# The second gather of an attention unit asked for one step later, and q loaded by ScalarE

## The chip, the cores and the metric

The kernel runs on one core of a Trainium2 chip. That core has five engines with an instruction stream each: TensorE (PE for its matmuls, PEld for its weight loads), VectorE (DVE), ScalarE (ACT), GpSimd (POOL) and SyncE (SP). Transfers between main memory and the core's memory run on 16 DMA engines; SyncE and ScalarE ask for plain ones, GpSimd for indirect ones (gathers). The metric is the device time of one execution in microseconds, smaller being better. A profile is of one further execution.

## The reference

Sparse attention, and then a layer of eight experts of which each row uses two:

```python
scores = scale * np.matmul(q, k.transpose(0, 1, 3, 2))     # batch 4, 8 heads, 768 rows, 64 wide
# a block of 32 rows sees its neighbours, the first and the last block, and 3 sampled blocks;
# the first and the last block of rows see everything
scores = np.where(mask, scores, -1000000000.0)
attn = softmax(scores)
x = np.matmul(attn, v)                                     # then rows of 512: 3072 x 512
logits = x @ w_gate
noisy_logits = logits + np.log1p(np.exp(x @ w_noise)) * noise
# the two best experts of a row, weights by a softmax over the two
h = np.maximum(x[mask] @ w1[e], 0.0)
out[mask] += top2_w[mask, k, None] * (h @ w2[e])
```

## The kernel before

Attention is cut into twelve units. A unit is a pair of batches and a group of 128 rows of each: six groups, two pairs. Five groups of a pair hold four blocks of 32 rows that see only eight blocks of keys each ("G"); one holds the first and last block (dense, "D") and two blocks more ("X"). A G unit has four macros: two batches times two halves of the heads. `Attention.steps` runs the macros as a pipeline, one step for each: in step n PE makes the scores of macro n (line 246, x32 matmuls), transposes the weights of macro n-1 (line 318), and multiplies those of macro n-2 with V (line 334, 64 matmuls, the groups named `va` and `vb` in turn). VectorE takes the row maxima of the scores (line 267) and norms the result (lines 376 to 382); ScalarE makes the exps (line 306) and copies the transposes (line 320). Routing of finished rows (lines 295 to 770) is slipped in between, in earnest from about step 28 on. After step 63 come the expert layers, which the change does not touch.

What a unit needs is fetched during the unit before it, by `ahead(n)`, which is called at the end of step n. For a G unit it consists of four gathers and four plain loads, and of keys and q:

- `gather_v(u, j)`, line 200: an indirect load of the sampled and near V rows of block j into `va`, 128 rows of 1040 floats, asked for by GpSimd. Ahead of each stands a 1x1 copy to `tick` (line 437) that reads VectorE's newest row maxima, so that GpSimd gets to the gather only when that step's maxima are made. `va` has two buffers, by the unit's parity; the first gather of a unit must wait until the unit before last has read its own.
- `load_v(u, j)`, line 194: a plain load of V windows into `vb`, asked for by ScalarE.
- `gather_k(u, bb)`, lines 211 to 216: twelve copies by GpSimd of sampled key blocks into `kg`, in the second step for the first batch and in the fourth for the second. `place_k` (line 236) is VectorE's part of it. The scores of the next unit read `kg`.
- `load_q(u)`, line 175: the q of the next unit, 512 KB, in the first step; `scale_q` (line 180) scales it on VectorE in the third.

Which gather stands in which step is set by `plan` (lines 414 to 421), where s is the first step of the unit that the V is for, so that s - 4 to s - 1 are the four steps of the unit before it. Every engine works its list in the order in which the program is written, and so does each queue of DMA requests. SyncE's list holds the finished rows (line 559, each waits for the norm), keys and V of the second pair of batches (lines 165 and 169), and q.

Of the kernel before, what the change touches and what calls it, by code (L numbers as in the profile page):

```python
# [40 lines left out]
class Attention:  # L41
# [130 lines left out]
    def load_q(self, k):  # L172
        hp, g = self.units[k]
        q = self.st["q", k] = self.qp.tile([P, self.BP, self.PR, P], F32, name="q")
        self.nc.sync.dma_start(q, self.qt[hp, g])

    def scale_q(self, k):

# [231 lines left out]
    def plan(self):  # L410

        self.values = {}
        for u in range(1, len(self.units)):
            s = self.first_step[u]
            for j in range(4):
                at = (s - 7 + 2 * j,) * 2
                if self.units[u - 1][1] != self.SPEC:
                    at = s - 3 + max(j - 1, 0), s - 3 + j
                for kind, n in zip("ab", at):
                    if kind == "b" or j < self.blocks(self.units[u][1]):  # L420
                        self.values.setdefault(n, []).append((kind, u, j))
# [1202 lines left out]
```

## Time and profile before

| what | us |
|---|---|
| median of three runs | 823.7 |
| lowest and highest | 817.61, 833.19 |
| profiled execution, its own time | 820.33 |
| its span, first to last instruction | 818.5 |
| attention's last steps end about | 283 |

The profile page gives each engine's busy time over the span. Further views group instructions by stretch, list them in order of time, or tell for one line how long its transfers took to land. In brackets behind a row of the timeline stands how long the engine was idle just before it and what ended that; "issue" there means that nothing the profile shows was waited for. The granted clock of TensorE is told as a share of 2.4 GHz; it has two levels, and 0.50 is the lower, 1.2 GHz.

### The profile page before, as it was taken

What the parts mean: (1) busy time and instruction counts of PE and PEld (TensorE: products, weight loads), DVE (VectorE), ACT (ScalarE), POOL (GpSimd) and SP (SyncE); (2) the same over time, 40 slices, a digit from 0 to 9 for tenths busy, and PEclk for the clock granted to TensorE, in tenths of its full rate; (3) what the DMA queues carried; (4) which work ended last, traced back from release to release, by engine and by line L of the source; (5) the groups of instructions that cost most, each with busy time, mean ns of one, the idle gap of its engine ahead of it and who ended that gap; (6) DMA issues with size and microseconds to landing.
All of it is one profiled execution on the core that took longest, in us unless ns stands there. A gap on an engine that the chain in (4) does not pass through costs nothing. (4 is left out here: it accounts for less than half of the span.)

```text
span 818.5 us, 21046 instructions
## 1 busy us (share of the span) xinstructions
PE 764.2 (93%) x8506; PEld 455.4 (56%) x8506; DVE 564.2 (69%) x1132; ACT 416.3 (51%) x729; POOL 333.7 (41%) x528
## 2 busy tenths in 40 slices
PE   5898989898998999999999999999999999999996
PEld 2566766775676775665445445444544544545542
DVE  5675659787897686426687786786787787785620
ACT  3574556455564542425375465554546546635620
POOL 4466565532366002423637327336335433333332
PEclk9999999899998899999999999999999999999999
DMA  9988788962486897979978378369359439343023
GB/s 358 341 278 285 246 310 289 324 222 67 134 260 213 169 326 255 184 177 164 286 143 222 89 126 235 95 111 222 85 84 236 132 65 190 99 100 48 1 41 56
DMA packets 122922, 148.66 MB, mean 182 GB/s; under 512 B 66111, under 2 KB 82751, under 8 KB 122816
## 3 DMA queue, kind: packets, MB, share of 16 engines
q1 hardware_dynamic: 97328, 75.76, 34.7%
q0 software_dynamic: 17600, 49.66, 25.3%
q10 hardware_dynamic: 7888, 21.81, 7.5%
q8 instruction: 69, 1.13, 0.5%
q14 instruction: 37, 0.30, 0.1%
HBM read 106.30 MB, written 27.00 MB: 163 GB/s over the span
## 5 line engine op out<-in xcount | busy, mean ns | idle before, releaser
L1160 POOL DMA_INDIRECT out_dram<-y,mt x56 | 85.7, 1530 | 260.7 <-ACT y L1155 121.2
L1099 PE MATMUL py<-w2h,hl 128*128 128x512 f16 x376 | 142.7, 380 | 0.8 <-DVE hl L1037 0.8
L1099 PE MATMUL py<-w2h,hh 128*128 128x512 f16 x376 | 142.8, 380 | 0.0
L1099 PE MATMUL py<-w2l,hh 128*128 128x512 f16 x376 | 142.7, 380 | 0.0
L1099 PEld LDWEIGHTS <-hh 128*128 128x128 f16 x752 | 72.9, 98 | 88.4 <-issue 2.5
L320 ACT ACTIVATE t<-t 128x512 f32<-128x512 f32 (+1 forms) x120 | 63.4, 568 | 80.3 <-PE t L318 79.7
L1055 PE MATMUL ph<-tx,w1a 128*128 128x408 f16 x384 | 99.0, 340 | 0.0
L1055 PEld LDWEIGHTS <-w1a 128*128 128x128 f16 x672 | 66.0, 98 | 58.0 <-issue 8.1
L1155 ACT ACTIVATE y<-py,r_tab 128x512 f32<-128x512 f32 (+1 forms) x49 | 33.6, 686 | 119.1 <-PE py L1099 102.1
L216 POOL COPY kg<-kv 128x128 f32 x264 | 68.4, 304 | 47.5 <-issue 15.1
L306 ACT ACTIVATE p<-s,nm 128x256 f32<-128x256 f32 x176 | 69.4, 480 | 25.5 <-DVE nm L267 24.8
L879 POOL TENSOR_TENSOR w2l<-wraw,w2h 128x1024 f16<-128x1024 f32 x24 | 51.7, 2152 | 62.5 <-ACT w2h L878 62.4
L318 PE MATMUL t<-ident,p 128*128 128x128 f32 x448 | 71.7, 302 | 4.9 <-ACT p L306 2.2
L960 POOL DMA_INDIRECT kv<-x_rows,gi x56 | 62.4, 1114 | 28.3 <-issue 12.1
L1037 DVE SCALAR_TENSOR_TENSOR hl<-ph,hh 128x408 f16<-128x408 f32 (+3 forms) x64 | 32.2, 525 | 58.3 <-ACT hh L1036 58.3
L318 PEld LDWEIGHTS t<-ident,p 128*128 128x128 f32 x448 | 52.1, 150 | 36.1 <-issue 16.6
L1036 ACT ACTIVATE hh<-area 128x408 f16<-128x408 f32 (+1 forms) x48 | 33.2, 713 | 72.6 <-DVE area L1059 72.6
L1055 PE MATMUL ph<-tx,w1b 128*128 128x408 f16 x192 | 65.2, 340 | 0.0
L1059 DVE TENSOR_TENSOR area<-ph,area 128x408 f32<-128x408 f32 x96 | 53.5, 578 | 15.7 <-PE ph L1055 11.1
L334 PE MATMUL po<-va,t 128*32 128x65 f32 x1408 | 49.5, 232 | 15.4 <-issue 8.7
L1099 PEld LDWEIGHTS <-hl 128*128 128x128 f16 x376 | 36.7, 98 | 45.6 <-DVE hl L1037 1.3
L267 DVE TENSOR_REDUCE nm<-s 128x4 f32<-128x1024 f32 (+1 forms) x48 | 54.2, 1129 | 8.5 <-PE s L246 8.4
(217 smaller groups left out, 1455.9 us busy)
## 6 DMA issues: line engine op xcount, KB each, us to landing
wraw<-in_moe_w_dram SPq DMA_DIRECT2D x64, 512.0 KB, 6.1
vb<-in_v_windows_dram ACTq DMA_DIRECT2D x16, 520.0 KB, 5.2
vb<-in_v_windows_dram ACTq DMA_DIRECT2D x24, 260.0 KB, 5.1
q<-in_q_dram SPq DMA_DIRECT2D x12, 512.0 KB, 9.0
out_dram<-zero ACTq DMA_DIRECT2D x8, 768.0 KB, 4.8
x_rows<-xr SPq DMA_DIRECT2D x19, 256.0 KB, 4.7
kv<-in_v_dram SPq DMA_DIRECT2D x2, 1560.0 KB
kv<-in_v_dram SPq DMA_DIRECT2D x6, 520.0 KB
```

The source lines that it names most:

```text
L216: nc.gpsimd.tensor_copy(KG[:, j, :, 32 * s:32 * s + 32], KT[:, :, bass.ds(offs[3 * j + s], 32)])
L267: red = lambda out, x: nc.vector.tensor_reduce(out, x, axis=AX.X, op=ALU.max, negate=True)
L306: self.nc.scalar.activation(p[:, 256 * u:256 * u + 256], S[:, a, 256 * r:256 * r + 256], AF.Exp, bias=nb[:, u:u + 1], scale=1.0 if k else ...
L318: self.nc.tensor.transpose(T[i][:, c:c + P], p[:, i * w + c:i * w + c + P], self.ident)
L320: self.nc.scalar.activation(t[:, i * w:(i + 1) * w], T[i][:, 0:w], AF.Copy)
L334: mm = lambda o, n, hl, l, r, start, stop: self.nc.tensor.matmul(O[o:o + n, hl], l, r, start=start, stop=stop, tile_position=(0, o))
L879: self.nc.gpsimd.tensor_tensor(lo, t, hi, op=ALU.subtract)
L960: g = nc.gpsimd.indirect_dma_start(out=self.xg[0:m, c], out_offset=None, in_=self.x_dram[0:nr], in_offset=bass.IndirectOffsetOnAxis(ap=r[" ...
L1055: nc.tensor.matmul(bank[:, 0:HC], self.wop[part][:, w, kb, fs], b(kb, a), start=start and n == 0, stop=n == 5, skip_group_check=True)
L1059: add = lambda e, out, p, q: e.tensor_tensor(out, p, q, op=ALU.add)
L1099: nc.tensor.matmul(py, h[:, f, o], w[x][:, f, :], start=i == 0, stop=i == last)
L1160: s = nc.gpsimd.indirect_dma_start(out=self.out, out_offset=bass.IndirectOffsetOnAxis(ap=r["mt"][0:m, c:c + 1], axis=0), in_=y[0:m], in_of ...
```

## The change

In `plan`, the steps of a G unit's gathers (those marked "a") become s-3, s-2, s-2, s-1 where they were s-3, s-3, s-2, s-1: the second gather is asked for in the third step of the unit before, not in its second. The plain V loads ("b") keep their steps, and so do the two units that follow a unit with dense rows. In `load_q` the loads of units 2 to 11 are asked for by ScalarE; those of units 0 and 1 stay with SyncE.

```diff
     def load_q(self, k):
         hp, g = self.units[k]
         q = self.st["q", k] = self.qp.tile([P, self.BP, self.PR, P], F32, name="q")
-        self.nc.sync.dma_start(q, self.qt[hp, g])
+        (self.nc.scalar if k > 1 else self.nc.sync).dma_start(q, self.qt[hp, g])
...
                 if self.units[u - 1][1] != self.SPEC:
-                    at = s - 3 + max(j - 1, 0), s - 3 + j
+                    at = s - 3 + (j + 1) // 2, s - 3 + j
```

GpSimd's list of before, in the second to fourth step of the first G unit (`tick` and `va` are the tick and the gather, line 211 loads the block numbers, 216 copies the keys; `nm` are a step's maxima, and the number tells the step):

```order
L437 COPY tick_100<-nm_876 1x1
L200 DMA va0_93<-in_v_dram,vidx_101 128x1040
L437 COPY tick_100<-nm_876 1x1
L200 DMA va0_93<-in_v_dram,vidx_101 128x1040
L211 TENSOR_LOAD koff_99
...
L437 COPY tick_100<-nm_988 1x1
L200 DMA va0_93<-in_v_dram,vidx_101 128x1040
L437 COPY tick_100<-nm_1069 1x1
L200 DMA va0_93<-in_v_dram,vidx_101 128x1040
L211 TENSOR_LOAD koff_99
```

GpSimd's list of the changed kernel at the same place:

```order
L437 COPY tick_100<-nm_876 1x1
L200 DMA va0_93<-in_v_dram,vidx_101 128x1040
L211 TENSOR_LOAD koff_99
...
L437 COPY tick_100<-nm_984 1x1
L200 DMA va0_93<-in_v_dram,vidx_101 128x1040
L437 COPY tick_100<-nm_984 1x1
L200 DMA va0_93<-in_v_dram,vidx_101 128x1040
L437 COPY tick_100<-nm_1069 1x1
L200 DMA va0_93<-in_v_dram,vidx_101 128x1040
L211 TENSOR_LOAD koff_99
```

One pair of tick and gather has moved from ahead of the first twelve key copies to behind them, and its tick reads the maxima of the third step.

ScalarE's list in the first step of a unit, as a piece of the difference (`q` is the moved load, `vb` the plain V load):

```order
 L306 ACTIVATE p<-s,nm 128x256 x4
 L194 DMA vb_95<-in_v_windows_dram 128x1040
+L175 DMA q<-in_q_dram 128x1024
 L320 ACTIVATE t<-t_1283 128x512
 L320 ACTIVATE t<-t_1284 128x512
```

The load of q stands behind the step's exps and V load and ahead of the next step's copies of transposes. From SyncE's list ten such loads are gone, each from behind finished rows and, in the first pair of batches, keys.

## Rows read from the trace of the kernel before

**Rows 1.** The page: busy time by engine, and the instruction queue (packets, MB, share).

```profile
PE 764.2 (93%) x8506; PEld 455.4 (56%) x8506; DVE 564.2 (69%) x1132; ACT 416.3 (51%) x729; POOL 333.7 (41%) x528
...
q8 instruction: 69, 1.13, 0.5%
```

**Rows 2.** Busy time by stretch: engines, then TensorE's clock, DMA share, GB/s.

```profile
0.00:180.00 180.00, 152.84 (x3586) 113.95 (x3587) 124.99 (x336) 95.08 (x216) 97.01 (x289) 0.94 0.85 298
...
135.00:152.00 17.00, 14.74 (x412) 11.42 (x413) 16.41 (x53) 9.43 (x23) 11.92 (x31) 1.00 0.97 342
...
235.00:252.00 17.00, 13.44 (x361) 9.90 (x361) 16.17 (x65) 9.35 (x22) 10.84 (x31) 1.00 0.91 309
```

**Rows 3.** PE's timeline, rows behind an idle time: start, length, instruction, idle before.

```profile
66.56 0.22 PE L334 MATMUL po<-vb,t 128*32 128x65 f32 x1 [2.27 <-issue]
...
77.55 0.32 PE L334 MATMUL po<-va,t 128*32 128x65 f32 x8 [1.23 <-issue]
...
83.62 0.27 PE L334 MATMUL po<-vb,t 128*32 128x65 f32 x2 [1.75 <-issue]
...
104.96 0.25 PE L334 MATMUL po<-va,t 128*32 128x65 f32 x2 [1.34 <-issue]
...
115.03 0.24 PE L334 MATMUL po<-va,t 128*32 128x65 f32 x1 [1.89 <-issue]
...
131.74 0.55 PE L318 MATMUL t<-ident,p 128*128 128x128 f32 x3 [0.75 <-issue]
...
151.89 0.25 PE L334 MATMUL po<-va,t 128*32 128x65 f32 x3 [1.96 <-issue]
...
253.32 0.32 PE L334 MATMUL po<-va,t 128*32 128x65 f32 x1 [1.94 <-issue]
```

**Rows 4.** DMA packets that start between 64.0 and 64.5 us: in all, and of instructions.

```profile
DMA packets 45, 0.19 MB, mean 376 GB/s; under 512 B 2, under 2 KB 2, under 8 KB 44
...
q8 instruction: 1, 0.02, 11.9%
```

**Rows 5.** Busy time by stretch behind two of PE's gaps, columns as in rows 2.

```profile
68.00:70.50 2.50, 2.50 (x32) 1.69 (x17) 2.50 (x4) 0.38 (x1) 2.17 (x3) 0.50 0.51 75
...
116.00:119.00 3.00, 3.00 (x34) 2.19 (x19) 2.42 (x4) 0.63 (x2) 1.97 (x9) 0.50 0.81 247
```

**Rows 6.** GpSimd's timeline, one unit: its four gathers and first key copies.

```profile
89.18 1.02 POOL L200 DMA_INDIRECT va<-in_v_dram,vidx  x1 [2.52 <-PE po L334]
...
90.88 1.03 POOL L200 DMA_INDIRECT va<-in_v_dram,vidx  x1 [0.16 <-issue]
93.30 3.39 POOL L216 COPY kg<-kv 128x128 f32 x12 [1.40 <-issue]
...
96.97 1.10 POOL L200 DMA_INDIRECT va<-in_v_dram,vidx  x1 [0.15 <-issue]
...
98.48 1.02 POOL L200 DMA_INDIRECT va<-in_v_dram,vidx  x1 [0.16 <-PE t L318]
```

**Rows 7.** PEld's timeline: scores that waited for GpSimd's key copies.

```profile
56.47 0.57 PEld L246 LDWEIGHTS s<-kg,q 64*32 64x32 f32 x20 [0.55 <-POOL kg L216]
...
96.74 0.57 PEld L246 LDWEIGHTS s<-kg,q 64*32 64x32 f32 x20 [0.20 <-POOL kg L216]
```

**Rows 8.** Timeline of a q load, ScalarE then, q's scaling; landings of q, of V loads.

```profile
98.47 0.60 SPq L175 DMA_DIRECT2D q<-in_q_dram  x1
...
99.52 0.52 ACTq L194 DMA_DIRECT2D vb<-in_v_windows_dram  x1
...
99.83 1.21 ACT L306 ACTIVATE p<-s,nm 128x256 f32<-128x256 f32 x3
...
110.55 0.75 DVE L180 TENSOR_SCALAR q<-q 128x1024 f32<-128x1024 f32 x1
...
DMA to landing us min/median/max: 9.0/9.0/9.0
...
DMA to landing us min/median/max: 3.3/5.1/7.7
```

## Prediction

> **What bounds the kernel now.** I read the page first. TensorE (PE) is busy 764.2 of 818.5 us [rows 1], so time is won only where PE stands idle or runs slowly. The change touches attention alone, so the next view is the busy time by stretch. In the first 180 us PE works 152.84 us at a granted clock of 0.94, the DMA engines are busy to 0.85 of their time, and neither VectorE (125 us) nor GpSimd (97 us) fills the stretch [rows 2]. From about 135 us on, routing joins in, and VectorE is busy 16.41 of 17 us and 16.17 of 17 us in the two densest stretches [rows 2]: what PE wins there, it may have to wait for again.
>
> Then I went down PE's own line for idle times. Eight gaps of 0.75 to 2.27 us are marked "issue", which is a wait for nothing that the profile names [rows 3]. They sit inside loops of matmuls whose operands have all arrived, some with a single matmul of a loop left. The DMA queues tell what they are. Queue q8 carries instructions: 69 packets of 1.13 MB together [rows 1], or 16.4 KB each. PE's matmuls and weight loads are 17,012 instructions, so a packet is some 250 of them, about one attention step. One packet starts between 64.0 and 64.5 us, among packets of all three data queues [rows 4], and PE, idle since 64.3, resumes at 66.56. I read this as a late block of instructions: PE has used up what it holds, and the request for the next block waited behind data. The price can be more than the gap: after the gap that ends at 66.56 the granted clock is 0.50 for 2.5 us, and after that at 115.03 for 3.0 us [rows 5], which is 1.2 GHz, the lower level. That costs half of each, 1.25 and 1.5 us.
>
> Last comes GpSimd's line in one unit [rows 6]. The first two gathers go at 89.18 and 90.88, then twelve key copies from 93.30, then the other two at 96.97 and 98.48. So the four are asked for as two pairs: GpSimd runs late behind its copies, and the third gather starts as soon as these are done.
>
> **The change, part by part.** *(a) GpSimd's order.* The second tick and gather leave the place ahead of the key copies. These then start earlier by 90.88 + 1.03 - 89.18 - 1.02 = 1.71 us [rows 6]. The next unit's first scores read what they copy, and two of these wait for it, 0.55 us and 0.20 us [rows 7]. Both waits go: **-0.75 us**. The moved gather starts near 95.3 us, behind the copies, so the third and fourth start when they did and the second set of copies too. GpSimd's total is the same. Nothing waits for the moved gather by itself, since the loop that reads it also reads the fourth, which is not moved. The tick ahead of it now waits for the maxima of the unit's third step; the copies cover that wait, and behind it are queued only the gathers and the second set of copies. So the requests become one and then three in a row, not one, two, one.
>
> *(b) q on ScalarE.* Ten of the twelve q loads move. SyncE asked for this one at 98.47; on ScalarE it stands behind the exps and the V load of the step, whose own issue takes 0.52 us from 99.52, so it goes at 100.04, 1.6 us later [rows 8]. Issuing it took 0.60 us on SyncE [rows 8], so until 100.64. The exps already handed to ScalarE last until 99.83 + 1.21 = 101.04, so the issue lies under them: **0 us**. Without that cover it would be 10 x 0.60 = 6 us. When does q land? The V loads that ScalarE issues land after 5.1 us (median), the one q load with a recorded landing took 9.0 [rows 8]. That gives 105.1 to 109.0, and the first reader, VectorE's scaling of q, runs at 110.55 [rows 8]: no wait at either end, though the margin falls to 1.5 us. On SyncE what stands behind q goes 0.6 us earlier, and no engine waits for them there.
>
> *(c) What stands ahead of the instruction blocks.* This is the larger and less certain part. A gather moves 128 x 1040 x 4 = 532 KB, which at the 376 GB/s of [rows 4] is 1.4 us of all DMA engines. It leaves the traffic after the first pair and joins that after the second. Nine pairs of the first kind are in the trace, and five are followed by a gap 5 to 8 us later: those that end at 77.55, 115.03, 131.74, 151.89 and 253.32 [rows 3]. Taking up to 1.4 us from each gives 1.23 + 1.4 + 0.75 + 1.4 + 1.4 = 6.2 us. If gaps under 1.4 us leave the clock alone, three falls of the clock go as well, 1.5 us each by [rows 5]: 10.7 us at most. Of this 4.1 us (77.55; 115.03 with its clock) lie before routing. The other 6.6 us lie where VectorE is nearly full, and I count a quarter of them, 1.6. Together **-5.7 us**, with 0 and -10.7 as the bounds.
>
> Against it, three of the eight second pairs are followed by a gap today: those that end at 66.56, 83.62 and 104.96 [rows 3]. Each grows by 1.4 us, and the last, at 1.34 + 1.4, would now bring the clock down (1.25 us): **+5.4 us**. In the other five units the block comes in time now; a third gather could cost each nothing, or a gap and its clock, 1.4 + 1.5 us, 14.5 us in all. I take nothing for them, since the moved q load takes 512 KB out of the same stretch for 1.6 us.
>
> A page of the Trainium skill speaks here. "Runtime: NRT & Kernel Launch", in its section on instruction fetch mechanics, says that the sequencer fetches the next 256-instruction block over a DMA queue of its own while it executes the current one, so that crossing a block is "mostly hidden". In this trace it is not, by the gap ending at 66.56. By the page part (c) would be nothing, and the sum -0.75 us.
>
> **The sum.** -0.75 - 5.7 + 5.4 = -1.1 us. The profiled execution took 820.33 us, so 819.3. It lies 3.4 us under the median of the three runs, 823.7, and with that distance the sum is 822.6. I forecast **821 us**, between the two: no change that can be told from the spread of the runs.
>
> **The rivals.** *The broken pair pays.* One gather ahead of the blocks is harmless, three are no worse than two, and VectorE takes up what PE wins: -0.75 - 10.7 = -11.4, so 809 us. For it: five of nine first pairs are followed by a gap. Against it: the three largest of its terms lie where VectorE is full.
>
> *Three gathers in a row are worse.* They ask for 4.2 us of the DMA engines' full rate at once, just where x_rows, keys and V of the next step are asked for. From the point where a block comes 1.4 us late or more in each of the five units without a gap after the second pair, the clock falls too, and the change loses: -0.75 - 4.1 + 5.4 + 14.5 = +15.1, so 835 us. For it: DMA engines at 0.85 of their time. Against it: bytes per unit are the same, and q moves off. A rule of the Trainium skill would rule this case out: "DMA: Bandwidth & Descriptors", under queues, rings and completion order, has each DMA engine take turns between the queues packet by packet, so a block would wait for a turn and not for all that is queued. No row here settles that.
>
> *q comes late.* If a load on ScalarE took 10.5 us, past its margin, each further microsecond would stop VectorE ten times: at 11.5 us +10, so 830 us. Against it: no load of this size took over 9.0 us.
>
> **How the numbers follow.** The forecast has a chance of 0.59 (814 to 827 us), the paying pair 0.18, three in a row 0.18, late q 0.05. The range that leaves out 2 in 10 is 809 to 835 us; it takes in the times of all the cases. About 2% is what a measurement of this kernel can tell from no change, 807.2 and 840.2 us around the median. The first needs more than the whole of the paying pair, 0.05; the second more than the whole of three in a row, 0.06; within 2% remains 0.89.
>
> **What would show it.** In the changed kernel's GpSimd line one gather should go before the copies and three behind them, and the copies should start about 1.7 us sooner after the first gather. PE's two waits for key copies should be gone. Among PE's "issue" gaps those 5 to 8 us after the lone gather should shrink, and those after the three grow. The q loads' issue should lie under exps, and VectorE should not wait ahead of the scaling of q. I am wrong if gaps of PE move by more than 10 us in total one way, if ScalarE stops at a q load's issue, or if a wait for a gather appears at the matmuls that read it.

## The result and the profile after

The changed kernel took 825.53 us (median of 20 executions, 821.39 to 835.38), the kernel before 822.06 us in the same comparison (20 executions). The ratio is 1.0051, with a 95% interval of 1.0026 to 1.0075: some 4 us slower, less than 2% but clear of the noise. The ratio leaves out the few executions that took over 1.5% longer than the fastest of their kernel. The forecast was 821 us and no change that can be told; the range, 809 to 835 us, holds the time. The profiled execution of the changed kernel took 827.67 us, its span 825.5 us.

The page shows the same work as [rows 1], busy times and the instruction queue alike:

```profile
PE 763.7 (93%) x8506; PEld 454.0 (55%) x8506; DVE 563.8 (68%) x1132; ACT 417.1 (51%) x729; POOL 335.4 (41%) x528
...
q8 instruction: 69, 1.13, 0.5%
```

Busy time by stretch, columns as in [rows 2] (the first 180 us and the two stretches of before):

```profile
0.00:180.00 180.00, 150.46 (x3495) 109.29 (x3495) 122.19 (x328) 94.65 (x215) 97.17 (x289) 0.96 0.85 293
...
135.00:152.00 17.00, 15.75 (x420) 11.99 (x410) 15.46 (x51) 9.57 (x23) 9.36 (x29) 1.00 0.93 312
...
235.00:252.00 17.00, 13.09 (x326) 9.84 (x327) 10.43 (x38) 8.90 (x23) 8.80 (x22) 0.90 0.76 236
```

In the first 180 us PE got through 3495 matmul records where it had 3586, from 135 to 152 us through 420 for 412, and in the last stretch through 326 for 361. The last matmul with V ends at 293.3 us and not at 282.7. So the time is lost inside attention; what follows is 3.8 us shorter in this profile than in that of before (532.1 and 535.9 us). GpSimd's timeline of the unit that answers to [rows 6] shows where the gathers went:

```profile
86.52 1.02 POOL L200 DMA_INDIRECT va<-in_v_dram,vidx  x1 [0.90 <-PE po L334]
89.90 3.36 POOL L216 COPY kg<-kv 128x128 f32 x12 [2.37 <-issue]
93.21 0.18 POOL L437 COPY tick<-nm 1x1 f32<-1x1 f32 x1
93.54 1.02 POOL L200 DMA_INDIRECT va<-in_v_dram,vidx  x1 [0.15 <-issue]
94.57 0.18 POOL L437 COPY tick<-nm 1x1 f32<-1x1 f32 x1
94.91 1.03 POOL L200 DMA_INDIRECT va<-in_v_dram,vidx  x1 [0.16 <-issue]
95.94 0.18 POOL L437 COPY tick<-nm 1x1 f32<-1x1 f32 x1
96.27 1.02 POOL L200 DMA_INDIRECT va<-in_v_dram,vidx  x1 [0.16 <-issue]
```

One gather, twelve copies, three gathers 1.37 us apart. PEld's timeline of the same microseconds has something that the profile of before has nowhere from 42 to 285 us:

```profile
93.70 0.44 PEld L334 LDWEIGHTS po<-vb,t 128*32 128x32 f32 x7
94.72 0.11 PEld L334 LDWEIGHTS po<-vb,t 128*32 128x32 f32 x1 [0.58 <-issue]
94.74 0.16 PEld L334 LDWEIGHTS po<-va,t 128*32 128x32 f32 x4
95.47 0.16 PEld L334 LDWEIGHTS po<-va,t 128*32 128x32 f32 x4 [0.57 <-issue]
96.21 0.17 PEld L334 LDWEIGHTS po<-vb,t 128*32 128x32 f32 x4 [0.57 <-issue]
96.93 0.15 PEld L334 LDWEIGHTS po<-vb,t 128*32 128x32 f32 x4 [0.56 <-issue]
97.18 0.14 PEld L246 LDWEIGHTS s<-kg,q 64*32 64x32 f32 x2
```

PE does not stop once and go on, as in [rows 3]. It gets four weight loads and their four matmuls, waits for nothing that is named (0.57 us on the line of the weight loads, 0.39 to 0.44 us on PE's own), gets the next four, and so on every 0.73 us, from within the first of the three gathers until 97.18, where the last of them ends (96.27 + 1.02 = 97.29). I call an idle time of 0.50 to 0.64 us of this kind, ahead of PEld's scores or V groups, a short gap, and one of 0.65 us or more, ahead of any weight load, a long one. Waits of 0.70 to 0.85 us ahead of the transposes (line 318) are left out; up to four of them stand in a profile. From 42 to 285 us the profile of before has no short gap and 17.4 us of long ones; that of the changed kernel 16 short ones, 9.2 us, and 13.8 us of long ones.

Of PE's long gaps these answer to the ones in [rows 3] that end at 66.56, 77.55 and 151.89; the last row is new, in a routing step:

```profile
66.87 0.22 PE L334 MATMUL po<-vb,t 128*32 128x65 f32 x1 [0.66 <-issue]
...
76.63 0.32 PE L334 MATMUL po<-va,t 128*32 128x65 f32 x8 [1.36 <-issue]
...
153.72 0.25 PE L334 MATMUL po<-va,t 128*32 128x65 f32 x3 [1.85 <-issue]
...
161.43 0.80 PE L763 MATMUL po<-r_val,r_hot 128*128 128x126 f32 x3 [3.08 <-issue]
```

Of waits for key copies only one is left in attention. It does not answer to [rows 7]: before had it too, at 49.05, and the copies that it waits for have no moved gather ahead of them. The scores that answer to the row at 56.47 wait no more. PEld's timeline of before, then of the changed kernel:

```profile
49.05 0.57 PEld L246 LDWEIGHTS s<-kg,q 64*32 64x32 f32 x20 [0.48 <-POOL kg L216]
```

```profile
49.47 0.57 PEld L246 LDWEIGHTS s<-kg,q 64*32 64x32 f32 x20 [0.50 <-POOL kg L216]
...
56.17 0.72 PEld L246 LDWEIGHTS s<-kg,q 64*32 64x32 f32 x32
```

And ScalarE with its new load, twice: under exps, as eight of the ten are, and the one that ScalarE stops for. (The tenth begins under exps, at 178.56, and ends while ScalarE waits for PE.)

```profile
102.06 0.60 ACTq L175 DMA_DIRECT2D q<-in_q_dram  x1
102.28 1.21 ACT L306 ACTIVATE p<-s,nm 128x256 f32<-128x256 f32 x3
...
246.06 0.60 ACTq L175 DMA_DIRECT2D q<-in_q_dram  x1
246.71 0.60 ACT L320 ACTIVATE t<-t 128x512 f32<-128x512 f32 x1 [0.56 <-issue]
```

### The profile page after: what moved, and what is told of

It is laid out like the page before. It is cut to its first block, busy times and chain, and to the rows that moved or that the text cites. A ratio compares the mean times of both kernels' runs of the same rounds, so it can differ in the third digit from the quotient of the medians.

```text
span 825.5 us, 21038 instructions
## 1 busy us (share of the span) xinstructions
PE 763.7 (93%) x8506; PEld 454.0 (55%) x8506; DVE 563.8 (68%) x1132; ACT 417.1 (51%) x729; POOL 335.4 (41%) x528
## 4 chain that ended last, share of the span: by engine, by line
PE 78%; DVE 10%; issue 4%; ACT 3%; DMA 3%; another core or an unknown queue 1%; POOL 0%; ACTq 0%; SPq 0%; POOLq 0%; DVEq 0%
PE py L1099 29%; PE ph L1055 18%; PE po L334 7%; PE s L246 6%; PE ph L1011 5%; PE t L318 5%; PE py L1110 3%; DVE area L1059 2%; PE pe L581 2%; DVE nm L267 1%; DMA va<-in_v_dram,vidx 1%; PE po L763 1%; PE pe L569 1%; DMA kv<-in_k_dram 1%; DMA xta<-kv 1%
## 5 line engine op out<-in xcount | busy, mean ns | idle before, releaser
L1160 POOL DMA_INDIRECT out_dram<-y,mt x56 | 87.7, 1566 | 257.0 <-ACT y L1155 124.0
L216 POOL COPY kg<-kv 128x128 f32 x264 | 70.0, 316 | 49.0 <-issue 17.4
L306 ACT ACTIVATE p<-s,nm 128x256 f32<-128x256 f32 x176 | 69.6, 481 | 20.8 <-DVE nm L267 19.9
L318 PE MATMUL t<-ident,p 128*128 128x128 f32 x448 | 69.5, 296 | 8.6 <-ACT t L320 3.7
L1055 PE MATMUL ph<-tx,w1b 128*128 128x408 f16 x192 | 64.5, 336 | 0.0
L246 PE MATMUL s<-kg,q 64*32 64x256 f32 x1408 | 56.7, 399 | 7.1 <-DVE kg L236 2.9
```

Of the source, the lines that this page charges most:

```text
L216: nc.gpsimd.tensor_copy(KG[:, j, :, 32 * s:32 * s + 32], KT[:, :, bass.ds(offs[3 * j + s], 32)])
L246: mm = lambda out, l, r, pos: nc.tensor.matmul(out, l, r, start=True, stop=True, tile_position=pos)
L306: self.nc.scalar.activation(p[:, 256 * u:256 * u + 256], S[:, a, 256 * r:256 * r + 256], AF.Exp, bias=nb[:, u:u + 1], scale=1.0 if k else ...
L318: self.nc.tensor.transpose(T[i][:, c:c + P], p[:, i * w + c:i * w + c + P], self.ident)
L1055: nc.tensor.matmul(bank[:, 0:HC], self.wop[part][:, w, kb, fs], b(kb, a), start=start and n == 0, stop=n == 5, skip_group_check=True)
L1160: s = nc.gpsimd.indirect_dma_start(out=self.out, out_offset=bass.IndirectOffsetOnAxis(ap=r["mt"][0:m, c:c + 1], axis=0), in_=y[0:m], in_of ...
```

## The experiments

Two theories stood at the start. **A**: gathers in a row make PE's instruction blocks late. **B**: the q load on ScalarE costs.

All results in one table. Ratios are to the kernel before, measured beside it on the same chip. The clock is the mean granted clock over the executions (their count behind it); before had 0.984 to 0.986 on each of the chips. Gaps are of the one profiled execution, 42 to 285 us. The chips are lettered in the order of their use; that of the first two profiles is not known, and before itself has no profile that is known to be from A to D. Each chip was used at one time, so that chip and time cannot be told apart. The last column needs no bound on gaps: it is how many matmuls PE started for each microsecond while GpSimd worked on a gather, and for each other microsecond, from 42 to 285 us.

| kernel | chip | ratio, 95% interval | clock | short gaps, us | long gaps, us | matmuls per us under a gather / else |
|---|---|---|---|---|---|---|
| the change | ? | 1.0051, 1.0026 to 1.0075 | 0.981 (19) | 16, 9.2 | 9, 13.8 | 14.8 / 21.8 |
| gathers only | A | 1.0043, 1.0014 to 1.0071 | 0.982 (11) | 14, 8.0 | 12, 15.6 | 14.8 / 21.8 |
| q only | A | 0.9994, 0.9975 to 1.0014 | 0.983 (12) | 4, 2.3 | 14, 21.4 | 16.2 / 21.5 |
| four in a row | A | 1.0118, 1.0080 to 1.0156 | 0.978 (6) | 27, 15.1 | 6, 9.5 | 13.0 / 21.3 |
| copies first | A | 0.9988, 0.9956 to 1.0020 | 0.982 (12) | 15, 8.7 | 7, 8.6 | 14.6 / 22.5 |
| thin, order of before | B | other routing | | 21, 12.2 | 5, 5.5 | 13.6 / 22.5 |
| thin, three together | B | other routing | | 21, 12.2 | 5, 7.3 | 14.7 / 22.5 |
| three spaced | B | 0.9916, 0.9878 to 0.9955 | 0.987 (9) | 8, 4.6 | 10, 15.6 | 17.9 / 21.8 |
| interleaved | B | 0.9940, 0.9907 to 0.9973 | 0.984 (12) | 12, 7.0 | 10, 12.7 | 17.2 / 21.2 |
| two extra gathers | C | 1.0293, 1.0259 to 1.0326 | 0.975 (6) | 27, 15.5 | 8, 15.4 | 12.0 / 22.2 |
| pair together, late | C | 1.0057, 1.0028 to 1.0086 | 0.984 (10) | 19, 10.8 | 11, 16.1 | 15.2 / 21.7 |
| three together, late | C | 1.0052, 1.0021 to 1.0083 | 0.982 (9) | 23, 13.1 | 9, 11.8 | 14.5 / 21.7 |
| pair apart | D | 1.0031, 0.9990 to 1.0073 | 0.988 (11) | 0 | 10, 18.0 | 19.3 / 21.5 |
| the change, three apart | E | 0.9991, 0.9954 to 1.0027 | 0.987 (12) | 2, 1.2 | 6, 7.8 | 21.0 / 21.4 |
| the change, three late | E | 1.0031, 0.9997 to 1.0064 | 0.988 (11) | 0 | 9, 11.6 | 23.7 / 20.8 |
| before again | E | 1.0017, 0.9985 to 1.0049 | 0.984 (10) | 0 | 10, 19.4 | 19.2 / 21.5 |
| the change again | E | 1.0032, 0.9997 to 1.0067 | 0.984 (12) | 1, 0.6 | 12, 20.9 | 20.5 / 21.2 |
| four in a row again | E | 1.0003, 0.9969 to 1.0037 | 0.984 (12) | 2, 1.1 | 10, 14.2 | 22.7 / 20.9 |
| two extra gathers again | E | 1.0025, 0.9992 to 1.0058 | 0.985 (10) | 1, 0.5 | 13, 21.9 | 21.4 / 21.1 |

The profiled execution of "three together, late" was the longest of its kernel, 833.19 us. In the profile of before the last column is 19.9 / 21.4, as on chips D and E, and in that of the change as on A to C: the two may come from different chips, and that one has the drip and the other not may in part be the chip's doing. Kernels of one chip are the safer comparison.

**Which half of the change costs.** Gathers only:

```diff
-                    at = s - 3 + max(j - 1, 0), s - 3 + j
+                    at = s - 3 + (j + 1) // 2, s - 3 + j
```

> The gathers in steps 2, 3, 3, 4; q stays with SyncE. Theory A (three gathers in a row make blocks of PE's instructions late): the whole loss, +3 to +5 us on the kernel before. Theory B (the q loads on ScalarE cost, by their issue on ScalarE's list or by their place among the transfers): -1 to +1 us.

q only:

```diff
-        self.nc.sync.dma_start(q, self.qt[hp, g])
+        (self.nc.scalar if k > 1 else self.nc.sync).dma_start(q, self.qt[hp, g])
```

> q on ScalarE; the gathers as before, in steps 2, 2, 3, 4. Theory A: -1 to +1 us. Theory B: the whole loss, +3 to +5 us, with ScalarE's copies of transposes or its V loads seen later behind the q load's issue.

The gathers alone gave 1.0043, q alone 0.9994. B falls. The step of q moves nothing, and it does not make up for anything either: the change whole (1.0051) costs no less than its gathers. On this chip the order of before has 4 short gaps (the kernel with q only) and the changed order 14; their gaps, short and long, add up to the same, 23.7 and 23.6 us.

**More and fewer in a row.** Three of the four gathers in the third step, so that all four stand behind the copies in most units:

```diff
-                    at = s - 3 + max(j - 1, 0), s - 3 + j
+                    at = s - 3 + max(j - 1, 1), s - 3 + j
```

> The gathers in steps 3, 3, 3, 4, so all four stand behind the key copies; q stays with SyncE. Theory A: worse than three in a row, +5 to +9 us. Theory B: -1 to +1 us, since no q load moves.

It gave 1.0118, some 10 us and a little more than the 5 to 9 forecast, and 27 short gaps, the most of the four kernels on that chip: the dose goes with A. Copies ahead of the gathers:

```diff
+        if k + 1 < nu and g != self.SPEC and i == half - 1:
+            self.place_k(k + 1, 0)
+            self.gather_k(k + 1, 0)
...
-            if i in (half - 1, 2 * half - 1):
+            if i == 2 * half - 1 or g == self.SPEC and i == half - 1:
```

> As before, but in a unit's second step GpSimd's key copies stand ahead of the tick and the first gather, so that GpSimd is not late and the ticks pace the gathers. Theory A: the gathers go one or two at a time with a step between, PE's waits for instructions shrink, -2 to -5 us. Theory B says nothing of the gathers' order: -1 us, from the waits for key copies alone.

No change (0.9988) where A had 2 to 5 us less, with 15 short gaps, in runs of three and four gathers here and there, and only 8.6 us of long ones. So A missed here, and the count of short gaps alone does not set the time.

**Bytes or GpSimd's work.** Thin gathers fetch an eighth of each row, in the order of before and in the changed one:

```diff
-        src = self.v.rearrange("h r w -> (h r) w")
+        W = self.VW // 8
+        src = self.v.rearrange("h r (e w) -> (h r e) w", w=W)
...
-            out=self.VA[k % 2][:, j], out_offset=None, in_=src,
+            out=self.VA[k % 2][:, j, 0:W], out_offset=None, in_=src,
```

> The order of before, with an eighth of each gather's bytes: a descriptor fetches 130 floats of a row and not 1040, so x is wrong wherever V comes from the gathered rows; 128 rows, the count of gathers and GpSimd's own time for each stay. It is the base of the thin kernel with the new order, and says by itself whether gathered bytes stand ahead of PE's instruction blocks. If bytes do (theory M1), most of the 17 us of long gaps in 42 to 285 us go, with the half clock behind them: 820.3 - 10 = about 810 us. If it is the number of descriptors or GpSimd's writing of them (theory M2), the long gaps stay: 820 us.

> The same thin gathers in the changed order (one gather, copies, three gathers); x is wrong in the same way. To be compared with the thin kernel in the order of before, not with the kernel before. M1, bytes asked for at once hold PE's instruction blocks back: nothing is left of the trickles (fewer than 3 short gaps of 0.50 to 0.64 us, where the full gathers have 14) and the two thin kernels are within 1.5 us of one another. M2, three gathers issued back to back hold them back whatever they carry: 8 or more short gaps, and 4 us longer than the thin kernel in the order of before.

Both kernels leave out seven eighths of each gathered row and fill `va` with ones at the start. With another x rows go to other experts, so the whole times (1670.83 and 1667.94 us) say nothing, and only attention is compared. From the first V matmul to the last it took 264.6 and 264.0 us (263.8 in the profile of before, whose chip is not known): with an eighth of the bytes the order makes no difference. Long gaps are 5.5 and 7.3 us where before had 17.4, as bytes would have it (M1). But both kernels have 21 short gaps, where M1 had none and M2 a difference between the two: each theory misses one half. Every one of the 42 lies in time with a gather on GpSimd. So I counted over the profiles of the change and of the kernels on chips A to C: of 207 short gaps, 195 overlap a gather instruction on GpSimd and 7 more begin within 0.3 us behind one, while these instructions fill 48 of the 243 us in before's order (20%; a stretch of 0.57 us put anywhere would overlap one in 29% of cases). (The count of 119 of 127 in an expectation below is mistaken; by then it was 134 of 138.)

**Gathers without bytes.** Two extra gathers of 130 floats a row, ahead of each unit's third:

```diff
+                for e in range(2 * (j == 2)):
+                    src = self.v.rearrange("h r (e w) -> (h r e) w", w=130)
+                    self.nc.gpsimd.indirect_dma_start(
+                        out=self.fill[:, e], out_offset=None, in_=src,
...
```

> The order of before, with two extra gathers of 130 floats a row ahead of each G unit's third one, into a scratch tile that nobody reads: four indirect loads in a row behind the key copies, of which two carry an eighth of the bytes (0.07 MB each). All that the reference needs is still computed. To be compared with the kernel that clears a scratch tile for as long at the same place. If GpSimd's own work on a gather is what slows PE's instruction supply (theory M2: 119 of 127 short gaps so far lie inside or within 0.3 us behind a gather on GpSimd, in thin kernels too), there are 10 short gaps or more, and the time is 3 to 8 us above the kernel with the clearings. If only the bytes asked for at once count (theory M1), the two are within 2 us of one another.

and its control, GpSimd busy for as long with clearings:

```diff
+                for _ in range(6 * (j == 2)):
+                    self.nc.gpsimd.memset(self.fill, 0.0)
```

> The order of before, with six clearings of a scratch tile (some 2.9 us by the 0.50 us that one took) ahead of each G unit's third gather: the pair behind the copies stays a pair, later by 2.9 us. The control for GpSimd's lost time. If gathers side by side are what costs and a late pair does no harm, the time is that of before within 2 us, with PE's waits for kg at the second set of copies as the only addition. If the three spaced gathers won time because they came later, not because they stood apart, this one wins too: 4 us or more below before.

844.64 us against the control's 824.64: 20 extra gathers cost 20 us, 1 us each, with 1.3 MB of bytes in all. On this chip M1 falls and M2 is left. But M2 had 3 to 8 us, the control has 19 short gaps itself, and the 8 more add 4.7 us only; between the two profiles, which differ by 17.9 us, 11.3 lie from the first V matmul to the last. Not all of the cost is read. Whether it is GpSimd's work on a gather or its 128 requests among the transfers, no run here parts. GpSimd's timeline and PEld's of the kernel with the extra gathers show it:

```profile
59.43 1.03 POOL L441 DMA_INDIRECT fill<-in_v_dram,vidx  x1 [0.15 <-issue]
60.77 1.01 POOL L441 DMA_INDIRECT fill<-in_v_dram,vidx  x1 [0.30 <-issue]
62.08 1.00 POOL L201 DMA_INDIRECT va<-in_v_dram,vidx  x1 [0.30 <-issue]
...
63.42 1.03 POOL L201 DMA_INDIRECT va<-in_v_dram,vidx  x1 [0.16 <-issue]
64.45 2.89 POOL L217 COPY kg<-kv 128x128 f32 x12
```

```profile
62.77 0.18 PEld L335 LDWEIGHTS po<-vb,t 128*32 128x32 f32 x5 [0.52 <-issue]
63.53 0.14 PEld L335 LDWEIGHTS po<-va,t 128*32 128x32 f32 x3 [0.58 <-issue]
64.25 0.17 PEld L335 LDWEIGHTS po<-va,t 128*32 128x32 f32 x3 [0.58 <-issue]
65.01 0.14 PEld L335 LDWEIGHTS po<-va,t 128*32 128x32 f32 x2 [0.58 <-issue]
65.07 0.19 PEld L335 LDWEIGHTS po<-vb,t 128*32 128x32 f32 x8
```

The weight loads come two to five at a time. The gathers end at 64.45, and from 65.07 on eight weight loads come in 0.1 us again. Under the first two gathers nothing of the kind is seen; I read it that PE drips only if it needs instructions while a gather runs. What the control itself cost, 1.0057, I had not expected; of M2 it shows nothing.

**Together or apart.** The changed order with clearings between the three, and a kernel that puts key copies between all gathers:

```diff
+                for _ in range(3 * (j > 1)):
+                    self.nc.gpsimd.memset(self.fill, 0.0)
                 self.nc.gpsimd.tensor_copy(self.tick, self.seen[0:1, 0:1])
```

> The changed order of gathers with full bytes, but GpSimd first clears a scratch tile three times (about 1.4 us in all by the 128x512 clearing of 0.53 us) ahead of each unit's third and fourth gather, so that the three behind the copies start some 2.7 us apart and not 1.36. If it is their standing back to back that costs (M1 and M2 both), the short gaps fall from 14 to 4 or fewer, and the time from 824.8 to 817 to 821 us. If it is the place of the moved gather (theory P: it now meets other data), the short gaps stay at 10 or more and the time at 824 us or above. GpSimd has 2.8 us more per unit; if the key copies then come late, PE's waits for kg show it by name.

```diff
         for j in range(n):
+            if j == n // 2 and between:
+                between()
             for s in range(3):
```

(`between` is the unit's second, or fourth, tick and gather.)

> The steps of before, but the second gather of a G unit stands between the first six and the last six key copies of the first set, and the fourth gather between the halves of the second set, so that no two gathers are neighbours in GpSimd's list except where GpSimd runs late. q stays with SyncE. If gathers close together are what makes PE's blocks late, in both forms (long gaps behind pairs, short ones behind three), both shrink: the long ones from 17 us to 8 or less with no short ones, and 0.75 us of waits for key copies: 812 us. If only a run of three or more matters, the pairs' long gaps stay: 819 to 820 us. If the order of gathers does not matter to the blocks at all but bytes per unit do, 820 us with the same gaps. Slower than 822 us would say that a gather between copies delays the keys.

Both beat before on that chip: 817.96 and 817.76 us against 823.97. The spaced one is in its forecast; it has 8 short gaps where 4 or fewer were forecast. The interleaved one missed its 812 us and had 12 short gaps where it was to have none. Four of the 8 and six of the 12 lie at five gathers in a row that fetch rows for the expert layers (from 262.8 and from 261.1 us), which neither edit parts; the others come singly. So the reason for the gain is only partly shown. The control, all clearings ahead of the three (six of them where j is 1):

> The changed order (one gather, copies, three gathers), with the six clearings ahead of the three instead of between them: the same GpSimd work as in the kernel with three spaced gathers, and the three back to back. If standing apart is what won there, this one is slower than before by 3 to 5 us, as the changed order alone was (ratio 1.0043), with 10 short gaps or more. If coming later is what won, it is 4 us or more below before, like the spaced one (ratio 0.9916).

1.0052, and 23 short gaps: with equal GpSimd work, three apart won 0.84% and three together lost 0.52%, though on two chips. A pair kept late cost as much (1.0057), so a run of two already costs there, or lateness does. The pair set apart (six clearings where j is 3):

> The order of before, with the six clearings of some 2.9 us between each G unit's third and fourth gather, where the control kernel had them ahead of both: the same GpSimd work, the same delay for the fourth gather and the second set of key copies, but the pair stands apart. The first pair of each unit stays together. The control came out at a ratio of 1.0057, as slow as the one with three together (1.0052), which the theory of neighbours did not expect. If neighbours cost from two on, this one is at least 4 us faster than the control, at a ratio of 1.001 or less. If it is GpSimd's lost time, which makes the fourth gather and the key copies late, this one is as slow as the control, 1.003 to 1.008, and the spaced three won by something else.

1.0031, at the edge of the second forecast, and its interval holds both: inconclusive. But its profile had no short gap at all, and before took 810.9 us beside it, not 820 to 824. To put the change with its three apart and together on one chip:

> The changed kernel whole (gathers and q), with three clearings of a scratch tile (some 1.5 us) ahead of each unit's third and fourth gather, so that the three behind the copies stand apart. In the same call as its control. If standing together is what the change costs, it is 4 us or more faster than the control and no slower than before (ratio 1.000 or less). If the gain of the spaced kernel of an earlier call (0.9916) was that call's chance, the two are within 2 us of one another and both near the change's own 1.005.

> The control: the changed kernel whole with the six clearings ahead of the first of the three, which stay together. The same GpSimd work in total, and the fourth gather and the second set of copies late by the same. If standing together costs: 1.004 to 1.009, and 4 us or more above its partner. If not: within 2 us of it.

0.9991 and 1.0031, intervals that overlap, medians 0.55 us apart (813.60 and 814.15), and 2 and 0 short gaps although the control keeps its three together. On this chip standing apart wins nothing, as was forecast if the earlier gain had been chance. The chip was now the suspect.

**The chip.** Four kernels that had run elsewhere, on one chip:

> The kernel before, unchanged, profiled on the same chip as the three kernels beside it. The short gaps of 0.50 to 0.64 us differ by chip: in every profile from three chips there are 4 to 28 (pairs 4 to 21), in those from two other chips 0, 0 and 2, the three kept together among them, and the kernel before takes 811 to 813 us there and not 820 to 824. Theory C (chip): the first profile of before, with none, came from a chip of the second kind, and on a chip of the first kind this one shows 4 to 20. Theory O (order): before has none on any chip.

> The changed kernel, unchanged, on the same chip. If the change's cost is made by the short gaps and these are the chip's, it is 1.003 to 1.007 where short gaps show and 0.998 to 1.002 where none do. If the cost has nothing to do with them, 1.003 to 1.007 on either kind of chip.

> All four gathers in a row behind the copies, on the same chip; 1.0118 and 27 short gaps where it ran first. On a chip with short gaps: 1.008 to 1.016 again, and more short gaps than the two kernels beside it. On a chip without them: within 0.4% of before, if short gaps make the cost; 1.008 or above, if something else does.

> The order of before with two extra small gathers in each unit; 1.0293 and 28 short gaps where it ran first. On a chip with short gaps: 1.025 or more. On a chip without them: the extra gathers cost only their queue and GpSimd's lost 2.7 us a unit, 1.003 to 1.008 as the clearings did, if PE's supply during a gather is what made the 2.9%; still 1.02 or more, if not.

On this chip before takes 811.92 us, there are 0 to 2 short gaps, and the costs go: four in a row from 1.0118 to 1.0003, two extra gathers from 1.0293 to 1.0025. From the first V matmul to the last these two take 255.8 and 257.8 us in their profiles, where it was 277.3 and 283.1. The last column of the table says the same without gaps: while a gather runs, PE starts 12.0 to 17.9 matmuls per us on A to C and in the first profile of the change, and 19.2 to 23.7 on D and E; else it is 20.8 to 22.5 everywhere. GpSimd's timeline of the four in a row, and PEld's "issue" waits of the same stretch, here:

```profile
92.64 1.02 POOL L200 DMA_INDIRECT va<-in_v_dram,vidx  x1 [0.64 <-PE pe L581]
...
94.00 1.32 POOL L200 DMA_INDIRECT va<-in_v_dram,vidx  x1 [0.16 <-issue]
...
95.67 1.02 POOL L200 DMA_INDIRECT va<-in_v_dram,vidx  x1 [0.16 <-issue]
...
97.28 1.02 POOL L200 DMA_INDIRECT va<-in_v_dram,vidx  x1 [0.41 <-PE pe L569]
```

```profile
93.38 0.18 PEld L334 LDWEIGHTS po<-vb,t 128*32 128x32 f32 x7 [0.18 <-issue]
...
95.43 0.85 PEld L318 LDWEIGHTS t<-ident,p 128*128 128x128 f32 x8 [1.16 <-issue]
...
96.89 0.16 PEld L334 LDWEIGHTS po<-va,t 128*32 128x32 f32 x8 [0.17 <-issue]
...
98.06 0.16 PEld L334 LDWEIGHTS po<-va,t 128*32 128x32 f32 x5 [0.19 <-issue]
```

Three of the four gathers take as long (1.02 us, the other 1.32), PE's weight loads wait once for more than 1 us (1.16), and nothing drips. The change itself gave 1.0032 with an interval of 0.9997 to 1.0067; before against itself gave 1.0017, 0.9985 to 1.0049. On this chip no cost of the change can be told.

## Why the prediction was wrong

**Part (a), GpSimd's order**, came as described: one and then three in a row. The key copies start 89.90 - 86.52 - 1.02 = 2.36 us behind the lone gather, not 1.40 as assumed, so that they came 0.74 us sooner behind the gather's start and not 1.71. It was enough: both waits of [rows 7] went. (A third of 0.48 us, which [rows 7] does not list, stayed; no gather moved ahead of it.) The -0.75 us stand.

**Part (b), q on ScalarE**, held: 0 us predicted, 0.9994 measured. The issue took 0.33 to 0.66 us and stopped ScalarE once in ten, for 0.56 us; VectorE did not wait ahead of scaling q.

**Part (c) holds the step that failed**: "In the other five units the block comes in time now; a third gather could cost each nothing, or a gap and its clock ... I take nothing for them, since the moved q load takes 512 KB out of the same stretch". The reason was no reason: with q in its old place the gathers cost the same (1.0043 and 1.0051). With the term at zero, the gathers came to -0.75 - 5.7 + 5.4 = -1.05 us; measured alone they cost 824.49 - 820.84 = +3.65 us (means), so if the other terms stood, this one was worth 4.7 us of its 0 to 14.5. The change went the way of the rival "three gathers in a row are worse", at a quarter of its 15.1 us.

Its form was another, too. I had a longer gap per unit and then half clock. The profile of the changed kernel shows a drip: 16 short gaps that add up to 9.2 us, 13 of them under or just behind a run of three. It does not look like a block whose request waited behind data, which was the mechanism of (c): the drip comes with an eighth of the bytes as well.

The two terms that were counted can be followed, since PE's program is the same and its gaps come back at the same matmuls. In three profiles of the order of before (before, before again, q only) the five gaps that were to shrink (those of 0.3 us or more) add up to 7.8, 10.2 and 7.1 us on PE's own line; in three of the changed order (the change, the change again, gathers only) to 4.2, 5.1 and 4.8. That is 3.7 us less on average, of 6.2 forecast. The three that were to grow add up to 5.4, 0 and 2.1 us, and then to 0.7, 4.8 and 1.9: no growth. So of the 5.4 us nothing showed in gaps, and the term at zero was worth more like 4.4 us (if the shrinking was worth nothing in time) to 8.1 (if all of it was). Five of nine, or three of eight, was one throw of dice: each gap comes in some profiles and not in others.

The clock was misread for the same reason. The profiled execution of before had a mean granted clock of 0.971; over 28 executions on chip A it is 0.985. I counted on falls of the clock that the change would take away, from an execution that had twice as many as usual. Over executions the clock is lower with the change, 0.981. An estimate, as if PE set the pace throughout: half speed costs one minus the clock, 825.5 x 0.0194 = 16.0 us with the change and 820.8 x 0.0151 = 12.4 us before, 3.6 us of the 4 lost. For four in a row it is 5.9 of 10.0 us, for the two extra gathers 9.1 of 23.5. For the spaced and the interleaved kernel it gives 2.2 of 6.0 and none of 4.9 us. By this estimate the clock is part of the cost on chips A to C, and not all.

Another estimate is the matmul time lost under gathers, from the last column of the table (the gathers' time, some 48 us, times one minus the ratio of the two rates): gathers only loses 3.6 us more than q only, and the time is 3.7 us longer (means); four in a row 6.3 for 10.0; two extra gathers 15.5 more than the late pair, for 19.3. Copies first loses 4.5 us more than q only and takes as long. Each rests on one profile a kernel.

The rule of the Trainium skill in "Runtime: NRT & Kernel Launch", instruction fetch mechanics, that crossing a block is "mostly hidden", would have left -0.75 us. The profile of before has long gaps against it, up to 2.27 us [rows 3]. Neither the rule nor the trace of before had the drip in it; it shows in 4 to 27 places on chips A to C.

**Shown, and not.** Shown: the cost lies in the gathers and not in q; on chips A to C PE starts fewer matmuls while GpSimd works on a gather (12.0 to 17.9 per us for 21.2 to 22.5 else), whatever the gather's bytes; on chip E it does not (19.2 to 23.7 for 20.8 to 21.5), and the costs of four in a row and of extra gathers go with it. Argued only: that the change's own 4 us are made by this. The number of short gaps on chip A (14 for 4), the clock and the lost matmuls fit; chip E cannot tell, since the interval of the change there (0.9997 to 1.0067) holds both no cost and the whole of it. Open: what differs between the chips, where the rest of the 20 us of the extra gathers is, why a late pair cost 0.57% on chip C, and why copies first, with 15 short gaps, cost nothing.

## What to carry to other kernels

When PE shows "issue" waits inside a loop, lay GpSimd's line beside it: on three chips here PE got through less while a gather ran, though no wait names it, and clearings or copies between gathers won 0.6 to 0.8% on one of them (and nothing that can be told on a fourth chip). Count rare events over several executions before a term of a sum rests on them: the clock of one profiled execution was twice as far from full as the mean. And repeat a small difference on a second chip: 2.9% became 0.3% here.

## What was not expected of the hardware

During gathers on GpSimd (1.02 us each) PE was fed a few weight loads and matmuls at a time, four every 0.73 us in the profile of the change, on three chips (202 of 207 short gaps lie at a gather), also with an eighth of the bytes. On two others there were 0 to 2 such gaps in a profile; on one of these two, three of the programs were the change, four in a row and two extra gathers, which had 16, 27 and 27 elsewhere. Before takes 811 to 813 us (medians) on these two and 820 to 824 us on the three.
